# Diagonals spread by GpSimd instead of ScalarE for units 0 to 7 of a recurrent-attention and MLP kernel, with new engine sequences

## The chip, the cores and the metric

One core of a Trainium2 chip runs the whole program. The metric is the device time of one execution in microseconds, and lower is better. The kernel before takes 484.99 us (median of 3 runs, 484.72 to 485.08).

## What is computed

The reference has two parts. The first is a recurrence over 768 tokens for 4 batches and 8 heads of width 48: a state of 48x48 per head is multiplied by a decay `w` and takes in `k v`, and each token reads it with `r`, adding its own `k v` weighted by `u`. The second is an MLP on the 3072 tokens, with an ELU between.

```python
for t in range(S):
    cur = np.einsum('bhd,bhe->bhde', u[None] * kt, vt)
    y[:, :, t] = np.einsum('bhd,bhde->bhe', rt, state + cur)
    state = wt[:, :, :, None] * state + np.einsum('bhd,bhe->bhde', kt, vt)
...
h = x @ w_in                      # 384 -> 2048
g = np.where(h > 0.0, h, np.exp(np.minimum(h, 0.0)) - 1.0)
out = g @ w_out                   # 2048 -> 384
```

Each token's own term is `sum(r u k) v`. In matrix form it is the diagonal of a token by token matrix, and this diagonal is what the change is about.

## The kernel before

The tokens are cut into 24 **units** (unit 0 to 23), four to each of six chunks of 512 token columns. Units 0 to 3 hold 128 tokens of one batch (`whole`), the later ones two halves of 64 tokens. The MLP of a chunk goes over 16 blocks `f` of 128 hidden columns, in 103 steps in all. The first six blocks of chunk 0 are cut in two halves, so that they can begin when units 0 and 1 alone are done.

The names in the sequences are tasks, with the number of the unit, block or step behind the dot. Those that the prediction speaks of:

- `es.i`, `gs.i` (L461, L470, L471): two scans over the decays of unit i on VectorE, with a small reciprocal ahead of the second. `rh.i` (L476) multiplies k and r by them.
- `rkc.i` (L495) then `pd.i` (L500) then `md.i` (L504): for units 0 to 3 the sums r u k as a product on VectorE, a small matmul on TensorE into PSUM, and a copy to the SBUF tile `md` on ScalarE. For the later units `rk.i`, `rku.i`, `md.i` (L483, L486, L490) on VectorE give `md`.
- `sp.i`: the **spread**. It writes the 128 by 8 values of `md` onto diagonals in the tile `ams`, with zeros around them. Units 0 to 7 do it on ScalarE, `spread_act` (L518): eight instructions, each an identity matrix scaled by one column of `md`. Units 8 to 23 do it on GpSimd, `spread` (L529): two affine selects of 64x512 that read `md` broadcast.
- `s.i` (L563, L570): transposes and scores on TensorE. `mk.i` (L599, L601, L605), the **mask**: VectorE copies the scores above the diagonal from PSUM into `ams`. It needs `s.i` and `sp.i`. `v.i` (L550, L640): TensorE multiplies `ams` by the values and makes the state's update. `xf`, `xh`, `xl` copy its result into the MLP's input.
- `a.f`, `cc.f` (L235), `wh.f`, `wl.f` (L731): the weights of block f are unpacked and split into a high and a low part, on ScalarE and VectorE by turns. `wh.0` and `wh.1` are casts on GpSimd (L727). `big.f` (L734) is a check on the weights for which nothing on TensorE waits.
- `g1.n`, `g2.n` (L263, L267; L295, L298): the MLP's matmuls of step n. Between them `r1`, `r2` (ScalarE), `stt` (VectorE, L277, one input from PSUM), `gh` (ScalarE) and `gl` (VectorE, L285).

What sets the order is the table `SEQUENCE` (L80): one list of tasks for each engine and for the DMA queue on SyncE. An engine takes its tasks in the order of its list and waits at each for what it needs. A small planner (`Plan.order`, L170) merges the five lists into program order by the numbers in `COST`, and `hold` says how many buffers a tile has. `FILL` (L44) puts matmuls of ones on TensorE ahead of a task (`warm`, L424), 36 of them in the first 25 us; their result is not used.

```python
def spread_act(u_):
    am = diagonal(u_)
    for q in range(2):
        for p in range(NP):
            act(am[:, q, p], ident if u_["whole"] else ident_h, AF.Copy, scale=u_["md"][:, q, p:p + 1])
```

Of the kernel before, what the change touches and what calls it, by code (L numbers as in the profile page):

```python
# [95 lines left out]
rh.3 stt.3 wl.3 cc.4 es.4 es.5 gl.3 wl.4 cc.5 mk.3 stt.4 wl.5 stt.5 rk.4 gl.4 big.3 cc.6 stt.6 gs.4 gl.5 xl.3 gl.6 xl.2 rku.4 stt.7 md.4 stt.8 cc.7
wl.6 rh.4 stt.9 sc.4 rk.5 gl.9 cc.8 gs.5 rku.5 stt.10 md.5 stt.11 rh.5 wl.7 mk.4 wl.8 gl.11 gl.10 cc.9 sc.5 rk.6 stt.12 stt.13 xl.4 es.6 up.4 rku.6
gl.13 gl.12 cc.10 gs.6 mk.5 stt.14 wl.9 gl.14 rh.6 cc.11 stt.15 md.6 wl.10 rk.7 wl.11 cc.12 gl.15 stt.16 up.5 xl.5 rku.7 es.7 sc.6 cc.13 stt.17 wl.12
gl.16 mk.6 md.7 cc.14 gs.7 gl.17 sc.7 stt.18 rh.7 wl.13 stt.19 up.6 wl.14 es.9 gl.18 xl.6 cc.15 stt.20 es.8 gl.19 wl.15 rk.8 mk.7 sc.8 stt.21 gs.9
gl.20 gl.21 rk.9 rku.8 xl.7 gs.8 rku.9 rh.8 stt.22 md.8 md.9 rh.9 gl.22 up.7 stt.23 tn.9 es.10 rk.10 gl.23 sc.9 stt.24 gs.10 rh.10 gl.24 stt.25 tn.10  # L100
es.11 rk.11 gl.25 rku.11 mk.8 big.10 stt.27 stt.26 md.11 rku.10 md.10 up.8 gs.11 gl.27 gl.26 mk.9 sc.10 rh.11 es.12 stt.28 big.11 rk.12 gl.28 xl.8
stt.29 gs.12 big.2 stt.30 up.9 tn.11 mk.10 gl.29 sc.11 rh.12 stt.31 xl.9 es.13 gl.30 gl.31 wl.1 wl.0 rku.12 gs.13 md.12 es.14 rk.13 stt.32 gl.32
rku.13 up.10 stt.33 gs.14 gl.33 tn.12 stt.34 sc.12 rk.14 rh.13 xl.10 stt.35 mk.11 gl.34 md.13 rku.14 gl.35 es.15 big.9 tn.13 stt.36 mk.12 rh.14 gl.36
# [36 lines left out]
ld_w.0 ld_k.0 ubd ld_w.1 ld_k.1 raw.0 ld_v.0 ld_w.2 ld_k.2 raw.1 ld_v.1 ld_w.3 raw.2 raw.3 ld_k.3 raw.4 ld_v.2 ld_w.4 ld_w.5 raw.5 ld_v.3 raw.6  # L140
# [983 lines left out]
```

## Time and profile before

| | before |
|---|---|
| median of 3 runs | 484.99 us (484.72 to 485.08) |
| the profiled execution | 486.13 us |
| its span, first to last instruction | 484.4 us |
| TensorE busy | 475.7 us (98%) |
| VectorE busy | 359.1 us (74%) |
| ScalarE busy | 260.4 us (54%) |
| GpSimd busy | 40.7 us (8%) |
| granted TensorE clock | 1.000 over the span |

The profiled execution took 1.73 us more than its span, and 1.14 us more than the median of the runs. Busy shares are averages over stages: the first 40 us, in which weights are unpacked and the first units are made, are unlike the rest. A matmul that is in flight counts as busy, so TensorE is read here by its waits and by when a given matmul starts.

### The profile page before, as it was taken

The numbers are of one execution on the slowest core, as the hardware profiler recorded it, in microseconds if no ns is written. First come the engines' busy times: TensorE is split into PE (matmuls) and PEld (weight loads), VectorE is DVE, ScalarE is ACT, GpSimd is POOL, SyncE is SP. The second block draws the span as 40 slices with busy tenths as digits, with TensorE's granted clock in tenths as the row PEclk, the third lists the DMA queues.
The fourth block names the chain that finished last, engine by engine and source line by source line (L and its number), as shares of the span: only waits on it lengthen the run. The fifth ranks groups of instructions, "written<-read, shape, count | busy, mean of one in ns | idle before, by whom it ended". The sixth has DMA issues, their size and how long they took to land.

```text
span 484.4 us, 12143 instructions
## 1 busy us (share of the span) xinstructions
PE 475.7 (98%) x4978; PEld 395.3 (82%) x4978; DVE 359.1 (74%) x545; ACT 260.4 (54%) x535; POOL 40.7 (8%) x56
## 2 busy tenths in 40 slices
PE   9999999999999999999999999999999999999996
PEld 8888888878888787788788878888888888888885
DVE  7999999999899999979997896655426453333332
ACT  4998878856544443635343643536544343644442
POOL 3000000004011302012101101101001000000000
PEclk9999999999999999999999999999999999999999
DMA  8999477417485664855754747332521100100001
GB/s 276 363 319 293 149 250 244 146 41 205 89 260 129 187 141 117 241 146 104 209 156 107 216 101 207 89 87 81 133 59 39 38 2 1 65 2 0 0 2 66
DMA packets 75418, 64.91 MB, mean 134 GB/s; under 512 B 56976, under 2 KB 57360, under 8 KB 75360
## 3 DMA queue, kind: packets, MB, share of 16 engines
q1 hardware_dynamic: 74784, 63.33, 46.3%
q8 instruction: 39, 0.64, 0.6%
q10 hardware_dynamic: 576, 0.79, 0.5%
q14 instruction: 19, 0.16, 0.1%
HBM read 49.67 MB, written 8.13 MB: 119 GB/s over the span
## 4 chain that ended last, share of the span: by engine, by line
PE 75%; DVE 16%; issue 3%; DMA 3%; ACT 2%; DVEq 0%; POOL 0%; POOLq 0%
PE ph L267 32%; PE acc L298 31%; PE py L550 2%; PE px L570 2%; PE acc L426 2%; DVE ams L605 2%; DVE m L277 2%; PE px L550 2%; DVE gl L285 2%; DVE eg L461 2%; DMA w<-in_wkr_dram 1%; DVE k L476 1%; PE px L640 1%; DVE tops L734 1%; DMA k<-in_wkr_dram 1%
## 5 line engine op out<-in xcount | busy, mean ns | idle before, releaser
L271 ACT ACTIVATE m<-ph 128x512 f32<-128x512 f32 (+2 forms) x103 | 58.3, 567 | 102.0 <-PE ph L267 69.8
L267 PE MATMUL ph<-xh,w_l 128*128 128x512 f32 (+1 forms) x294 | 112.0, 381 | 0.0
L298 PE MATMUL acc<-gh,w_l 128*128 128x512 f32 (+1 forms) x292 | 111.2, 381 | 0.0
L277 DVE SCALAR_TENSOR_TENSOR m<-m,ph 128x512 f32<-128x512 f32 (+2 forms) x103 | 66.2, 646 | 57.2 <-ACT m L274 56.6
L281 ACT CAST gh<-m 128x512 fp32r<-128x512 f32 (+1 forms) x98 | 58.9, 602 | 86.6 <-PE acc L298 60.4
L267 PE MATMUL ph<-xh,w_h 128*128 128x512 f32 (+1 forms) x264 | 102.5, 388 | 1.8 <-DVE m L277 1.4
L298 PE MATMUL acc<-gh,w_h 128*128 128x512 f32 (+1 forms) x264 | 102.3, 388 | 0.0
L285 DVE TENSOR_TENSOR gl<-m,gh 128x512 fp32r<-128x512 f32 (+1 forms) x98 | 67.0, 690 | 46.3 <-ACT gh L281 45.1
L298 PE MATMUL acc<-gl,w_h 128*128 128x512 f32 (+1 forms) x264 | 100.4, 380 | 0.3 <-DVE gl L285 0.3
L267 PE MATMUL ph<-xl,w_h 128*128 128x512 f32 (+1 forms) x264 | 100.3, 380 | 0.0
L267 PEld LDWEIGHTS ph<-xh,w_l 128*128 128x128 f32 x294 | 55.3, 188 | 10.8
L298 PEld LDWEIGHTS acc<-gh,w_l 128*128 128x128 f32 x292 | 54.9, 188 | 10.5
L274 ACT ACTIVATE m<-m 128x512 f32<-128x512 f32 (+2 forms) x103 | 61.2, 601 | 1.7
L267 PEld LDWEIGHTS ph<-xh,w_h 128*128 128x128 f32 x264 | 49.6, 188 | 13.8 <-DVE m L277 3.3
L298 PEld LDWEIGHTS acc<-gh,w_h 128*128 128x128 f32 x264 | 49.6, 188 | 10.3
L298 PEld LDWEIGHTS acc<-gl,w_h 128*128 128x128 f32 x264 | 49.6, 188 | 9.7 <-DVE gl L285 0.7
L267 PEld LDWEIGHTS ph<-xl,w_h 128*128 128x128 f32 x264 | 49.7, 188 | 8.9
L529 POOL TENSOR_SCALAR_AFFINE_SELECT ams<-md 64x512 f32<-64x512 f32 x32 | 32.1, 1002 | 242.2 <-PE py L550 164.2
L461 DVE TENSOR_TENSOR_SCAN eg<-w,reset 112x520 f32<-112x520 f32 (+1 forms) x24 | 30.1, 1256 | 2.8 <-DMA w<-in_wkr_dram 2.8
L471 DVE TENSOR_TENSOR_SCAN eg<-w,reset 112x520 f32<-112x520 f32 (+1 forms) x24 | 30.3, 1263 | 0.8
L476 DVE TENSOR_TENSOR k<-k,eg 112x1024 f32<-112x1024 f32 x24 | 29.1, 1214 | 0.1
L605 DVE COPY_PREDICATED ams<-upper_h,px 64x512 f32<-64x512 uint32 x32 | 23.5, 735 | 1.4 <-PE px L570 0.9
(127 smaller groups left out, 501.6 us busy)
## 6 DMA issues: line engine op xcount, KB each, us to landing
wraw<-in_wraw_dram SPq DMA_DIRECT2D x16, 767.8 KB, 6.6
rk<-in_rk_dram SPq DMA_DIRECT2D x20, 384.0 KB, 4.5
k<-in_wkr_dram SPq DMA_DIRECT2D x13, 512.0 KB, 4.3
w<-in_wkr_dram SPq DMA_DIRECT2D x24, 227.9 KB, 4.1
k<-in_wkr_dram SPq DMA_DIRECT2D x11, 448.0 KB, 5.5
wide<-in_vp_dram SPq DMA_DIRECT2D x32, 128.0 KB, 4.0
...
```

Of the source, the lines that this page charges most:

```text
L267: nc.tensor.matmul(ph, w[f][:, 0, k], y[:, k], start=(k == n == 0), stop=(k == NK - 1 and n == 2))
L271: act(s["m"], s["ph"], AF.Relu, scale=-1.0)
L274: act(s["m"], s["m"], AF.Exp, scale=-1.0)
L277: stt_(s["m"], s["m"], -1.0, s["ph"], ALU.add, ALU.max)
L281: nc.scalar.copy(s["gh"], s["m"])
L285: nc.vector.tensor_tensor(s["gl"], s["m"], s["gh"].bitcast(F32), ALU.subtract)
L298: nc.tensor.matmul(a_, w[f][:, 1, m], fold(s, g[:, a:b]), start=(first and n == 0), stop=(final and n == 2))
L461: nc.vector.tensor_tensor_scan(out=eg[:, 0, 0:n][:, ::-1], data0=u_["w"][:, 1:n + 1][:, ::-1], data1=reset[:, 0, 0:n][:, ::-1], initial=0. ...
L471: nc.vector.tensor_tensor_scan(out=u_["eg"][:, 1, 1:n + 1], data0=u_["w"][:, 0:n], data1=reset[:, 1, 0:n], initial=0.0, op0=ALU.mult, op1= ...
L476: tt(t, t, u_["eg"][:, :, 0:u_["n"]].rearrange("d z (s t) -> d z s t", t=u_["L"] + 1)[..., 1:], ALU.mult)
L529: nc.gpsimd.affine_select(out=am[rs, h].rearrange("t q p s -> t (q p) s"), in_=u_["md"][rs].rearrange("t q p -> t (q p)").unsqueeze(2).bro ...
L605: nc.vector.copy_predicated(u_["am"][rs, h], above[L][rs], pa[rs])
```

## The change

The spread of units 0 to 7 moves from ScalarE to GpSimd. `spread_rows` writes units 0 to 3 with one affine select of 128x1024, and units 4 to 7 with two of 64x512. The sums `pd.i` get PSUM columns of their own, 448 to 463 of the bank `py`, two sets by turns, where before they shared columns 0 to 7 with the transposes. The task `s.i` no longer names `sp.i` among the tasks that it comes after; the mask `mk.i` still does. All five lists of `SEQUENCE` are new, and so is `FILL`, now 40 matmuls of ones.

```diff
-FILL = {("pd",0):17,("s",0):5,("pd",1):3,("s",1):2,("v",1):8,("s",2):1,("g2",0):0}
+FILL = {("pd",0):19,("s",0):3,("pd",1):2,("v",0):3,("v",1):10,("g1",1):3,("g2",0):0}
...
-SPREAD = ["ACT"] * 8 + ["POOL"] * 16
+SPREAD = ['ROWS'] * 8 + ['POOL'] * 16
...
     def diag_pe(u_):
-        u_["pd"] = pd = single()[:, 0:NS].rearrange("t (p z) -> t p z", p=NP)
+        lo = NP * R2 + NS * (u_["i"] % 2)
+        u_["pd"] = pd = single()[:, lo:lo + NS].rearrange("t (z p) -> t z p", p=NP)
         for p in range(NP):
-            nc.tensor.matmul(pd[:, p], u_["rkc"][:, p, :], ubd[:, p, :], start=True, stop=True)
+            nc.tensor.matmul(pd[:, :, p], u_["rkc"][:, p, :], ubd[:, p, :], start=True, stop=True)
...
-    def spread_act(u_):
-        am = diagonal(u_)
-        for q in range(2):
-            for p in range(NP):
-                act(am[:, q, p], ident if u_["whole"] else ident_h, AF.Copy, scale=u_["md"][:, q, p:p + 1])
...
+    def spread_rows(u_):
+        am, n = diagonal(u_).rearrange("t q p s -> t (q p) s"), u_["L"]
+        for lo in range(0, C, n):
+            rs = slice(lo, lo + n)
+            nc.gpsimd.affine_select(out=am[rs], in_=u_["md"][rs].rearrange("t q p -> t (q p)").unsqueeze(2).broadcast_to([n, NS, n]),
+                                    pattern=[[0, NS], [1, n]], compare_op=ALU.is_equal, fill=0.0, base=0, channel_multiplier=-1)
...
-                [("rh", i), ("const",)] + [("sp", i)] * (i > 1) + before * (not new))
+                [("rh", i), ("const",)] + before * (not new))
...
-            hold("pb", ("pd", i), [("md", i)], fifo=False)
+            hold("pd", ("pd", i), [("md", i)])
```

Three places show how the lists moved. The first is VectorE from `rh.3` to `mk.3`, the mask of unit 3, before:

```order
L476 TENSOR_TENSOR k_295<-k_295,eg_372 112x1024
L277 SCALAR_TENSOR_TENSOR m_463<-m_463,ph_441 128x256
L731 TENSOR_TENSOR w_l_103<-wg_435,w_h_102 128x768
L235 SCALAR_TENSOR_TENSOR wg_510<-wraw_299,top_117 128x768
L461 SCALAR_TENSOR_TENSOR eg_525<-w_325,reset_104 112x520
L461 SCALAR_TENSOR_TENSOR eg_545<-w_395,reset_104 112x520
L285 TENSOR_TENSOR gl_550<-m_463,gh_530 128x256
L731 TENSOR_TENSOR w_l_103<-wg_510,w_h_102 128x768
L235 SCALAR_TENSOR_TENSOR wg_568<-wraw_411,top_117 128x768
L599 COPY_PREDICATED ams_114<-upper_108,px_115 128x512 x2
```

and the same stretch now:

```order
L477 TENSOR_TENSOR k_282<-k_282,eg_345 112x1024
L278 SCALAR_TENSOR_TENSOR m_420<-m_420,ph_404 128x256
L278 SCALAR_TENSOR_TENSOR m_445<-m_445,ph_425 128x256
L730 TENSOR_TENSOR w_l_103<-wg_413,w_h_102 128x768
L236 SCALAR_TENSOR_TENSOR wg_487<-wraw_289,top_117 128x768
L462 SCALAR_TENSOR_TENSOR eg_504<-w_384,reset_104 112x520
L730 TENSOR_TENSOR w_l_103<-wg_487,w_h_102 128x768
L236 SCALAR_TENSOR_TENSOR wg_525<-wraw_387,top_117 128x768
L286 TENSOR_TENSOR gl_539<-m_445,gh_485 128x256
L598 COPY_PREDICATED ams_114<-upper_108,px_115 128x512 x2
```

One of the two scans (`es.4`) has gone behind the mask; `stt.2` has moved here from just ahead of `mk.2`. From the first scan to `mk.3` everything else is the same set of tasks.

The second place is VectorE's first unit, now (L462 and L472 are scans, L496 is `rkc`, L477 is `rh`):

```order
L462 SCALAR_TENSOR_TENSOR eg<-w,reset 112x516 x2
L471 RECIPROCAL reset<-eg 112x4
L472 SCALAR_TENSOR_TENSOR eg<-w,reset 112x516
L496 TENSOR_TENSOR rkc<-k 112x512
L477 TENSOR_TENSOR k<-k,eg 112x1024
L471 RECIPROCAL reset<-eg 112x4
L472 SCALAR_TENSOR_TENSOR eg<-w,reset 112x516
L496 TENSOR_TENSOR rkc<-k 112x512
L598 COPY_PREDICATED ams<-upper,px 128x512 x2
```

The first row's second instruction, `es.1`, now stands ahead of `gs.0` and `rkc.0`; before it stood behind both.

The third place is GpSimd's list behind its constants, now:

```order
L409 MEMSET st 112x1280
L521 AFFINE_SELECT ams<-md 128x1024 x2
L388 MEMSET reset 112x1040
L389 MEMSET reset 112x8
L521 AFFINE_SELECT ams<-md 128x1024 x2
L534 MEMSET wide 32x512
L521 AFFINE_SELECT ams<-md 64x512 x8
L534 MEMSET wide 32x512 x2
L528 AFFINE_SELECT ams<-md 64x512 x2
L726 CAST w_g<-wt 128x768
L528 AFFINE_SELECT ams<-md 64x512 x4
L726 CAST w_g<-wt 128x768
```

The rows at L521 are new there, and the two casts `wh.1` and `wh.0`, which stood one behind the other, now have two units' spreads between them.

## Rows read from the trace of the kernel before

**Rows 1.** Busy time by stretch: us, then each engine's busy us (x instructions), clock, DMA share, GB/s.

```profile
5.00:10.00 5.00, 5.00 (x39) 4.86 (x38) 4.90 (x8) 1.48 (x7) 0.00 (x0) 1.00 1.04 357
...
35.00:40.00 5.00, 4.01 (x66) 3.39 (x66) 5.00 (x10) 4.01 (x9) 0.00 (x0) 1.00 1.02 392
```

**Rows 2.** All of VectorE's waits in the first 100 us: total us, times, longest.

```profile
DVE eg L461 <- DMA w<-in_wkr_dram: 1.4, 1, 1.4
DVE reset L387 <- PEq L1111: 1.1, 1, 1.1
DVE ams L601 <- PE px L550: 0.6, 1, 0.6
```

**Rows 3.** All of TensorE's waits from 40 us on, same columns.

```profile
PE ph L267 <- DVE m L277: 1.4, 2, 1.0
PE px L550 <- issue: 1.0, 1, 1.0
PE ph L267 <- DVE reset L470: 0.2, 1, 0.2
```

**Rows 4.** Instructions at L518, the spread on ScalarE: duration min/median/max, and who waited.

```profile
L518 ACT ACTIVATE ams<-ident,md x32: 384/388/404, 8.8 to 32.4; 128x128 f32<-128x128 f32 x32
...
  ACT m L271: 0.4, 1
```

**Rows 5.** VectorE in order of time: start us, us, instruction.

```profile
6.50 0.67 DVE L495 TENSOR_TENSOR rkc<-k 112x512 f32<-112x512 f32 x1
...
9.55 1.23 DVE L471 TENSOR_TENSOR_SCAN eg<-w,reset 112x516 f32<-112x516 f32 x1
10.70 0.67 DVE L495 TENSOR_TENSOR rkc<-k 112x512 f32<-112x512 f32 x1
11.50 1.35 DVE L599 COPY_PREDICATED ams<-upper,px 128x512 f32<-128x512 uint32 x2
...
32.79 2.37 DVE L461 TENSOR_TENSOR_SCAN eg<-w,reset 112x520 f32<-112x520 f32 x2
35.07 0.40 DVE L285 TENSOR_TENSOR gl<-m,gh 128x256 fp32r<-128x256 f32 x1
...
37.13 1.35 DVE L599 COPY_PREDICATED ams<-upper,px 128x512 f32<-128x512 uint32 x2
```

**Rows 6.** TensorE and ScalarE in order of time: unit 0, and the values of unit 3.

```profile
7.53 0.95 PE L500 MATMUL py<-ubd,rkc 112*128 112x2 f32 x8
...
8.52 0.17 ACT L504 COPY md<-py 128x8 f32<-128x8 f32 x1 [6.41 <-PE py L500]
...
38.54 0.73 PE L550 MATMUL px<-ams,wide 128*32 128x128 f32 x17 [0.72 <-DVE ams L599]
```

**Rows 7.** Instructions at L529, the spread on GpSimd: duration min/median/max, first and last.

```profile
L529 POOL TENSOR_SCALAR_AFFINE_SELECT ams<-md x32: 651/657/2092, 111.7 to 367.1; 64x512 f32<-64x512 f32 x32
```

**Rows 8.** Groups of GpSimd's instructions: count, busy us, mean ns of one, idle before.

```profile
masks.py:199 POOL TENSOR_SCALAR_AFFINE_SELECT ident<-ident 128x128 f32<-128x128 f32 x1 | 0.3, 293 | 0.1
```

**Rows 9.** One spread and VectorE beside it, in order of time.

```profile
224.86 3.40 POOL L529 TENSOR_SCALAR_AFFINE_SELECT ams<-md 64x512 f32<-64x512 f32 x2 [16.41 <-PE py L550]
...
225.06 0.55 DVE L486 TENSOR_TENSOR rk<-rk,ub 128x384 f32<-128x384 f32 x1
225.53 0.68 DVE L285 TENSOR_TENSOR gl<-m,gh 128x512 fp32r<-128x512 f32 x1
226.13 1.68 DVE L461 TENSOR_TENSOR_SCAN eg<-w,reset 112x520 f32<-112x520 f32 x1
```

**Rows 10.** The two casts of GpSimd, VectorE beside them, and TensorE behind, in order of time.

```profile
162.66 2.06 POOL L727 CAST w_g<-wt 128x768 fp32r<-128x768 f32 x2
...
162.70 1.33 DVE L285 TENSOR_TENSOR gl<-m,gh 128x512 fp32r<-128x512 f32 x1 [0.74 <-ACT gh L281]
163.95 1.18 DVE L486 TENSOR_TENSOR rk<-rk,ub 128x384 f32<-128x384 f32 x1
...
166.25 0.50 PE L267 MATMUL ph<-xh,w_h 128*128 128x512 f32 x1 [0.98 <-DVE m L277]
```

More of the change, by code (lines that the diff above doesn't have):

```diff
@@ L96 @@
[L96 to L103, printed above, removed]
@@ L112 @@
-mk.22 gl.76 xl.21 stt.77 stt.78 up.21 gl.77 sc.23 gl.78 stt.79 least gl.79 stt.80 stt.81 gl.80 gl.81 mk.23 verdict stt.82 gl.82 xl.22 stt.84 stt.83
-gl.84 gl.83 stt.85 xl.23 stt.86 gl.85 gl.86 stt.87 gl.87 stt.88 gl.88 stt.89 gl.89 stt.90 gl.90 stt.91 stt.92 gl.91 gl.92 stt.93 gl.93 stt.94 stt.95
-gl.94 gl.95 stt.96 gl.96 stt.97 stt.98 gl.97 gl.98 stt.99 gl.99 stt.100 gl.100 stt.101 stt.102 gl.101 gl.102 end.1 end.2 end.3
+es.0 es.1 gs.0 rkc.0 rh.0 gs.1 rkc.1 mk.0 rh.1 es.2 cc.0 gs.2 rkc.2 mk.1 rh.2 stt.0 es.3 cc.1 gs.3 cc.2 xl.1 xl.0 stt.1 wl.2 cc.3 rkc.3 mk.2 rh.3
@@ new lines @@
+rh.8 gl.21 xl.7 rku.8 sc.8 rk.9 stt.22 up.7 md.8 es.10 gl.22 gs.9 rku.9 stt.23 rh.9 gs.10 stt.24 gl.23 tn.9 wl.1 gl.24 md.9 rh.10 sc.9 stt.25 mk.8
+gl.25 stt.26 es.11 tn.10 gs.11 rk.10 es.12 rk.11 stt.27 gl.26 rku.10 up.8 gs.12 mk.9 gl.27 stt.28 md.10 rh.11 stt.29 gl.28 xl.8 big.15 wl.0 rku.11
+es.13 tn.11 mk.10 stt.30 sc.10 md.11 gl.29 rh.12 gs.13 gl.30 stt.31 up.9 rk.12 stt.32 tn.12 rh.13 gl.31 rku.12 sc.11 es.14 big.11 xl.9 stt.33 gs.14
+gl.32 big.10 md.12 stt.34 gl.33 rk.13 mk.11 stt.35 rku.13 up.10 big.14 gl.34 tn.13 rh.14 stt.36 xl.10 es.15 gl.35 md.13 sc.12 rk.14 xl.11 up.11 gl.36
@@ L115 @@
+mk.22 stt.75 sc.23 gl.75 stt.76 gl.76 stt.77 gl.77 mk.23 stt.78 gl.78 stt.79 xl.22 stt.80 gl.79 stt.81 gl.80 stt.82 gl.81 gl.82 stt.83 least gl.83
+stt.84 gl.84 xl.23 stt.85 gl.85 stt.86 gl.86 stt.87 stt.88 gl.87 gl.88 stt.89 stt.90 gl.89 stt.91 gl.90 verdict stt.92 gl.91 gl.92 stt.93 gl.93 stt.94
+gl.94 stt.95 gl.95 stt.96 gl.96 stt.97 gl.97 stt.98 stt.99 gl.98 gl.99 stt.100 gl.100 stt.101 stt.102 gl.101 gl.102 end.1 end.2 end.3
 """,
     ACT="""
-md.0 pc.1 sp.0 pc.0 kt.0 a.0 md.1 sp.1 xf.0 up.0 kt.1 xh.0 r1.0 a.1 md.2 sp.2 r2.0 xf.1 a.2 r1.1 up.1 xh.1 r2.1 wh.2 a.3 pc.3 kt.2 r1.2 r2.2 pc.2 wh.3
@@ L135 @@
+r2.85 gh.84 r1.86 gh.85 r2.86 gh.86 r1.87 r2.87 gh.87 r1.88 r2.88 out.4.0 out.4.1 r1.89 gh.88 out.4.2 r2.89 r1.90 r2.90 gh.89 r1.91 r2.91 gh.90 gh.91
+r1.92 r2.92 r1.93 r2.93 gh.92 r1.94 gh.93 r2.94 r1.95 gh.94 r2.95 gh.95 r1.96 r1.97 r2.96 gh.96 r2.97 gh.97 r1.98 r2.98 r1.99 r2.99 gh.98 r1.100 gh.99
+r2.100 r1.101 gh.100 r2.101 r1.102 r2.102 gh.101 gh.102 part end.0
 """,
     POOL="""
-const reset.4 clear.0 clear.1 clear.2 sp.9 sp.8 sp.10 sp.11 sp.12 wh.1 wh.0 sp.13 sp.14 sp.15 sp.16 sp.17 sp.18 sp.19 sp.20 sp.21 sp.22 sp.23
+const sp.0 sp.1 reset.4 sp.2 sp.3 clear.0 sp.4 sp.5 sp.6 sp.7 clear.1 clear.2 sp.8 wh.1 sp.9 sp.10 wh.0 sp.11 sp.12 sp.13 sp.14 sp.15 sp.16 sp.17
@@ L138 @@
+sp.18 sp.19 sp.20 sp.21 sp.22 sp.23
 """,
     SP="""
[L140 to L142 removed]
@@ L150 @@
+ld_wx.2 store.3.1 ld_wx.4 ld_wx.6 store.4.1 store.4.2 guard store.4.0
 """,
```

121 lines of the change are left out of this document (58 added, 63 removed).

## The prediction

> **What bounds the kernel now.** I read the busy time by stretch first, then the waits of VectorE and of TensorE, and then the first 40 us in order of time. In the stretches [rows 1] look at the third busy number, VectorE: 4.90 of 5.00 us at 5 to 10 us, and all of 35 to 40 us. Its waits over the first 100 us [rows 2] are 3.1 us in all, and 2.5 of them come before it has a decay to scan. So from its first scan on VectorE has work at nearly every moment, and whatever the first units need from it comes when its list has got there. TensorE's busy number means less early, since it also runs matmuls of ones; what shows its state is the matmul of `v.3` at 38.54 us [rows 6], which waited for VectorE's mask `ams`, and the 35 to 40 us stretch [rows 1], where TensorE has 4.01 of 5.00 us. Behind it TensorE is full: all its waits from 40 us on are 2.6 us [rows 3]. Its work behind `v.3` is the same before and after the change.
>
> So the time is the moment of `v.3`, plus a fixed amount of TensorE work, plus its few waits. ScalarE, which the change relieves, sets none of these: of the 64 instructions of the spread there (32 of them 388 ns each), only 0.4 us of waiting hangs on them, and that is another ScalarE task [rows 4]. Eight make a unit, at most 8 x 0.388 = 3.1 us of ScalarE for each of the first four, and I give that relief **nothing**: the masks that need a spread come out of VectorE's list later than the spread is ready. The cover is VectorE's own backlog; were it gone, ScalarE's relief could be worth some tenths. That `s.i` no longer comes behind `sp.i` is worth nothing for the same reason, as are the PSUM columns of `pd.i`: both let TensorE be early for a mask that is late.
>
> **The change part by part.** I follow VectorE from its first scan to `mk.3`.
>
> *The moved scan.* `es.4` goes behind `mk.3`. Two scans started at 32.79 us and the next instruction at 35.07 us [rows 5], so one is 2.28 / 2 = 1.14 us. It has to be done before `gs.4`, well behind `v.3`, where TensorE has steps of its own to run: **-1.14 us**.
>
> *Unit 0.* `es.1` now stands ahead of `rkc.0`, so `rkc.0`, which ended at 6.50 + 0.67 = 7.17 us [rows 5], ends about 1.0 us later (a scan, less a pause that it fills), at 8.2 us. Its sums left TensorE at 7.53 + 0.95 = 8.48 us [rows 6], 1.3 us behind it, and the copy to `md` ended at 8.52 + 0.17 = 8.69 us [rows 6]; now that is 9.7 us, and the spread can ask at 9.8 us. I need the length of a 128x1024 select, which the trace doesn't show. A 128x128 one took 0.293 us [rows 8] and a 64x512 one at least 0.651 us [rows 7]; (0.651 - 0.293) / 384 columns is 0.93 ns each, so 1024 columns are 0.651 + 512 x 0.93 ns = **1.13 us** undisturbed, an estimate from these two rows.
>
> But it won't be undisturbed. The spreads' durations run from 0.651 to 2.092 us with the same shape [rows 7]. In [rows 9] a select that comes at 224.86 us, two in a row lasting 3.40 us, stands through a product of two SBUF tiles (225.06) and another (225.53); then the scan at 226.13 takes 1.68 us instead of the 1.23 us of [rows 5], 0.45 us more. The casts say it again [rows 10]: beside them `gl` takes 1.33 us, where the same kind at 225.53 took 0.68 us, and `rku` 1.18 us where it took 0.55 us at 225.06 [rows 9], so 0.65 and 0.63 us more, and TensorE then waits 0.98 us at 166.25 us. GpSimd reading SBUF and VectorE reading two SBUF tiles shut each other out, one instruction at a time. A mask or `stt` reads PSUM and one SBUF tile, and I take it as open to GpSimd.
>
> The spread of unit 0 comes at 9.8 us in the middle of `gs.1`, which runs from 9.55 us to 10.7 us, with `rkc.1` behind it [rows 5]. If it goes in between, it ends at 11.85 us, `rkc.1` at 12.3, and the mask starts at 12.35 us; if `rkc.1` passes it, it runs from 11.3 to 12.45 us and the mask starts at 12.5 us. Before, it started at 11.50 us [rows 5]. The Trainium skill (SBUF — State Buffer, Who interferes with whom) says that the two engines share a port pair as an exclusive lock, and that whichever issues first has it. The trace agrees on the lock; on the order [rows 9] differ, as a waiting select was passed by two products. By the page the term is +0.85, by the row +1.0, and the sum would differ by 0.15 us. I take **+0.9**. The lowest is +0.4 (in between, and `rkc.1` not held up), the highest +1.0.
>
> *Units 1 to 3.* A select that goes in between two port users costs VectorE its length less what an instruction start hides: 0.45 us of 0.65 us above, so about 0.2 us hidden, and 0.93 us here. For unit 1 there is hardly a way round: from `mk.0` to `mk.1` the list is `rh.1`, `es.2`, `cc.0`, `gs.2`, `rkc.2`, all port users: +0.9. Unit 2 can go in beside `stt.1` or where VectorE waits for ScalarE: +0.6. Unit 3 can hide under `mk.2` or under `stt.2`, `stt.3`, which now stand together: +0.3. Together **+1.8**; nothing at best, since half the selects so far were not stretched (the median of [rows 7] is 0.657 us), and 3 x 0.93 = 2.8 us at worst.
>
> `v.3` then comes 0.9 + 1.8 - 1.14 = 1.6 us later, at about 40.1 us.
>
> *Units 4 to 7.* Eight selects of 64x512, two per unit. Behind each `md` VectorE's next is an `stt`, under which the first can hide; the second meets port users and costs 0 to 0.45 us. At 0.2 us each that is 0.8 us of VectorE, and I pass half on to TensorE, which has some work ahead there: **+0.4**, between 0 and 4 x 0.45 = 1.8 us.
>
> *TensorE's waits behind 40 us.* The two casts are taken apart, so their 1.3 us no longer fall on one spot. Of the 1.4 us that TensorE waited for `stt` [rows 3], I give back **-0.6**. The 1.0 us put down to issue has no cause that I can see, and I leave it. The lists are new throughout, with the DMA queue's order: I can't follow 390 us of them, and bound this by all 2.6 us of [rows 3] gone, less 0.2, or by one more wait like that at 166.25 us: -2.4 to +1.2. The 4 more matmuls of ones, and the ten ahead of `v.1`, stand where TensorE waits for a mask.
>
> The sum is -1.14 + 0.9 + 1.8 + 0.4 - 0.6 = **+1.36 us**. Against the profiled execution (486.13 us, a span of 484.4 and 1.73 around it) that would be 487.5 us; the median of the runs lies 1.14 us under that execution, so I predict 484.99 + 1.36, **486.3 us**.
>
> **The rivals.** *VectorE is not held up (faster).* The selects find the masks, the `stt` and the small pauses, and GpSimd is the one that waits. For it: half of the 32 spreads were not stretched at all [rows 7]. Against it: those ran where VectorE also had masks, `stt` and reductions; the first 40 us are scans, products and unpacking. Then the front is -1.14 + 0.4 = -0.7, the waits behind it -0.6 to -2.4: about 483.1 us. It decides at the point where the delay of VectorE before `mk.3`, unit 0 included, is under 1.14 us.
>
> *A draw.* The delay just eats the moved scan, ScalarE's relief is worth nothing, TensorE was full behind 40 us and stays so: 485.0 us. For it: [rows 3]. A kernel whose TensorE waits so little can't gain much.
>
> *GpSimd is starved (slower still).* If it is passed again and again, as in [rows 9], each mask of units 1 to 3 stands and waits the whole 1.13 us, and those of units 4 to 7 0.65 us: -1.14 + 1.0 + 3.4 + half of 2.6 = +4.6, less the 0.6: 489.0 us. Against it: no select waited more than 1.5 us so far.
>
> *The change doesn't do what it says*, since ScalarE was no bound: that is the draw.
>
> **How the numbers follow.** About 0.2% (1 us) is what a measurement of this kernel can tell from no change. Chances: VectorE held up, as forecast, 0.36; starved 0.08; a draw 0.22; not held up 0.34. The forecast's own range, with the bounds of unit 0 and of the first three selects, is 485.2 to 488.2 us. For 8 in 10 I take in the faster case down to 482.8 us (front -0.7, waits -1.5) and go up to 488.5 us. Slower by over 0.2% has 0.44, within 0.2% 0.22, faster 0.34.
>
> **What would show it.** In the changed kernel's trace: a 128x1024 select of 1.13 us where nothing stands beside it, longer elsewhere; scans and products of VectorE in the first 40 us stretched from 1.23 or 0.67 us to about 2.0 or 1.5 us, three or four of them; `mk.0` at 12.3 to 12.5 us; `v.3` near 40.1 us against 38.54 us; the two casts apart with no wait of 1 us behind them; VectorE still without waits. If `v.3` comes before 38.5 us with no VectorE instruction stretched, the port term is wrong. If it comes at 40 us and the kernel is still no slower, the end is not set by `v.3`, and the new lists won it back later: then TensorE's waits behind 40 us are under 1 us.

## The result and the profile after

The changed kernel takes 490.18 us (median of 4 runs, 488.90 to 491.03), the kernel before 485.03 us in the same series (484.72 to 485.10). The ratio is 1.0106 (95% interval 1.0087 to 1.0125): slower by 5.15 us, where +1.36 us was forecast, and outside the range of 482.8 to 488.5 us. The profiled execution of the changed kernel took 488.90 us with a span of 486.8 us.

The busy time by stretch, in the columns of [rows 1]:

```profile
5.00:10.00 5.00, 4.11 (x36) 3.92 (x35) 4.74 (x8) 0.46 (x3) 0.30 (x1) 1.00 0.99 283
35.00:40.00 5.00, 4.70 (x43) 4.04 (x43) 5.00 (x7) 4.15 (x8) 1.28 (x1) 1.00 1.04 293
```

ScalarE at 5 to 10 us went from 1.48 to 0.46 us and GpSimd has work, so the change does what it says. VectorE still fills 35 to 40 us, but with 7 instructions where it had 10. GpSimd's select and VectorE beside it show why:

```profile
9.70 1.09 POOL L521 TENSOR_SCALAR_AFFINE_SELECT ams<-md 128x1024 f32<-128x1024 f32 x1 [4.86 <-ACT md L515]
14.27 1.50 POOL L521 TENSOR_SCALAR_AFFINE_SELECT ams<-md 128x1024 f32<-128x1024 f32 x1 [3.48 <-ACT md L515]
...
26.69 1.60 POOL L521 TENSOR_SCALAR_AFFINE_SELECT ams<-md 128x1024 f32<-128x1024 f32 x1
34.47 1.81 POOL L521 TENSOR_SCALAR_AFFINE_SELECT ams<-md 128x1024 f32<-128x1024 f32 x1 [6.18 <-ACT md L515]
```

```profile
9.71 2.17 DVE L472 TENSOR_TENSOR_SCAN eg<-w,reset 112x516 f32<-112x516 f32 x1
11.80 0.66 DVE L496 TENSOR_TENSOR rkc<-k 112x512 f32<-112x512 f32 x1
12.38 1.33 DVE L598 COPY_PREDICATED ams<-upper,px 128x512 f32<-128x512 uint32 x2
...
14.74 2.11 DVE L462 TENSOR_TENSOR_SCAN eg<-w,reset 112x516 f32<-112x516 f32 x1
...
27.45 1.65 DVE L730 TENSOR_TENSOR w_l<-wg,w_h 128x768 fp32r<-128x768 f32 x1
...
35.26 2.12 DVE L462 TENSOR_TENSOR_SCAN eg<-w,reset 112x520 f32<-112x520 f32 x1
...
39.35 1.35 DVE L598 COPY_PREDICATED ams<-upper,px 128x512 f32<-128x512 uint32 x2
```

VectorE's waits in the first 100 us are much as in [rows 2], but for new ones, of which these are the two longest; both come behind 40 us:

```profile
DVE m L278 <- ACT m L275: 1.0, 2, 0.6
DVE ams L600 <- POOL ams L521: 0.6, 1, 0.6
```

Each of the four selects stretches one VectorE instruction with two SBUF inputs: three scans (1.23 us undisturbed, [rows 5]) by 0.94, 0.88 and 0.89 us, and one split of weights (0.95 us undisturbed) by 0.70 us, 3.41 us in all. Less the 1.14 us of the moved scan that is 2.27 us. `v.3` starts at 40.81 us against 38.54 us [rows 6], 2.27 us later as well:

```profile
40.81 0.96 PE L549 MATMUL px<-ams,wide 128*32 128x128 f32 x26
```

All of TensorE's waits from 40 us on, in the columns of [rows 3], and the place of the first in order of time:

```profile
PE px L549 <- issue: 1.9, 1, 1.9
PE acc L299 <- DVE gl L286: 0.7, 1, 0.7
```

```profile
59.04 0.33 PE L549 MATMUL px<-k,st 48*32 48x64 f32 x8
61.30 0.42 PE L549 MATMUL px<-k,st 48*32 48x64 f32 x22 [1.93 <-issue]
```

The sum, 2.6 us, is that of before, but one wait of 1.9 us now stands inside `v.4`, in the midst of 30 like matmuls, and no engine ends it. A profiled execution is one of several: the four runs have mean granted clocks of 0.999, 1.000, 0.997 and 0.996 and take 488.90, 489.36, 491.00 and 491.03 us. The two with the lower clock are 2 us longer. The profiled one is of the first sort; and the profiled one of before lay 1.14 us above its median. So the pair of profiles shows 486.8 - 484.4 = 2.4 us of the 5.15.

### The profile page after: what moved, and what is told of

It is laid out like the page before. It is cut to its first block, busy times and chain, and to the rows that moved or that the text cites. A ratio compares the mean times of both kernels' runs of the same rounds, so it can differ in the third digit from the quotient of the medians.

```text
span 486.8 us, 12114 instructions
## 1 busy us (share of the span) xinstructions
PE 476.8 (98%) x4986; PEld 396.0 (81%) x4986; DVE 362.5 (74%) x545; ACT 242.7 (50%) x471; POOL 57.8 (12%) x68
## 4 chain that ended last, share of the span: by engine, by line
PE 85%; DVE 8%; DMA 3%; issue 2%; SPq 1%; ACT 0%; DVEq 0%
PE acc L299 38%; PE ph L268 37%; PE py L549 3%; PE px L569 2%; PE px L549 2%; PE px L639 1%; DMA k<-in_wkr_dram 1%; DVE k L477 1%; DVE eg L462 1%; DVE eg L472 1%; DVE m L278 1%; DMA rows<-turn 1%; DMA w<-in_wkr_dram 1%; DVE wg L236 1%; DVE w_l L730 1%
## 5 line engine op out<-in xcount | busy, mean ns | idle before, releaser
L286 DVE TENSOR_TENSOR gl<-m,gh 128x512 fp32r<-128x512 f32 (+1 forms) x98 | 65.5, 669 | 58.3 <-ACT gh L282 58.0
L528 POOL TENSOR_SCALAR_AFFINE_SELECT ams<-md 64x512 f32<-64x512 f32 x32 | 33.4, 1042 | 201.9 <-PE py L549 87.6
L462 DVE TENSOR_TENSOR_SCAN eg<-w,reset 112x520 f32<-112x520 f32 (+1 forms) x24 | 32.6, 1360 | 1.6 <-DMA w<-in_wkr_dram 1.6
L472 DVE TENSOR_TENSOR_SCAN eg<-w,reset 112x520 f32<-112x520 f32 (+1 forms) x24 | 31.7, 1321 | 0.8
L477 DVE TENSOR_TENSOR k<-k,eg 112x1024 f32<-112x1024 f32 x24 | 30.2, 1257 | 0.3 <-DMA k<-in_wkr_dram 0.3
```

The source lines that it names most:

```text
L286: nc.vector.tensor_tensor(s["gl"], s["m"], s["gh"].bitcast(F32), ALU.subtract)
L462: nc.vector.tensor_tensor_scan(out=eg[:, 0, 0:n][:, ::-1], data0=u_["w"][:, 1:n + 1][:, ::-1], data1=reset[:, 0, 0:n][:, ::-1], initial=0. ...
L472: nc.vector.tensor_tensor_scan(out=u_["eg"][:, 1, 1:n + 1], data0=u_["w"][:, 0:n], data1=reset[:, 1, 0:n], initial=0.0, op0=ALU.mult, op1= ...
L477: tt(t, t, u_["eg"][:, :, 0:u_["n"]].rearrange("d z (s t) -> d z s t", t=u_["L"] + 1)[..., 1:], ALU.mult)
L528: nc.gpsimd.affine_select(out=am[rs, h].rearrange("t q p s -> t (q p) s"), in_=u_["md"][rs].rearrange("t q p -> t (q p)").unsqueeze(2).bro ...
```

## The experiments

Two causes were to be told apart. **P**: GpSimd reading SBUF shuts VectorE out. **C**: TensorE waits in `v.4` for its own instructions, and then runs for a while at a lower clock. Against both stood **S**: the new sequences are worse in themselves. The texts on record say what each theory forecasts. All times, with ratios to the kernel before in the same series; its own median went from 484.96 to 485.72 us between the series, so kernels of different series are compared by their ratios. In the kernel before `v.3` starts at 38.54 us.

| kernel | median us (range, runs) | ratio to before (95%) | `v.3` starts, us |
|---|---|---|---|
| changed kernel | 490.18 (488.90 to 491.03, 4) | 1.0106 (1.0087 to 1.0125) | 40.81 |
| act_first_four | 490.82 (488.99 to 493.37, 6) | 1.0113 (1.0086 to 1.0140) | 41.32 |
| rows_in_old_lists | 490.08 (488.12 to 491.90, 6) | 1.0098 (1.0072 to 1.0124) | 40.69 |
| write_only_select | 487.51 (486.24 to 488.75, 12) | 1.0039 (1.0026 to 1.0052) | 37.80 |
| fewer_ones | 489.64 (488.12 to 490.74, 6) | 1.0080 (1.0057 to 1.0102) | 40.59 |
| v4_later | 488.53 (487.64 to 489.12, 6) | 1.0066 (1.0049 to 1.0083) | 40.54 |
| write_only_v4_later | 485.26 (484.62 to 488.56, 12) | 1.0006 (0.9991 to 1.0021) | 38.10 |
| select_twice | 492.87 (491.92 to 494.73, 5) | 1.0158 (1.0134 to 1.0182) | 43.75 |
| scan_behind_mask | 484.92 (484.81 to 486.61, 12) | 0.9996 (0.9984 to 1.0007) | 37.65 |
| scan_and_check_later | 485.46 (484.82 to 487.75, 12) | 1.0002 (0.9989 to 1.0014) | 37.68 |
| and_casts_apart | 485.51 (484.16 to 485.95, 11) | 1.0000 (0.9991 to 1.0010) | 37.79 |
| four_to_seven_in_old_lists | 486.88 (485.81 to 489.65, 12) | 1.0029 (1.0012 to 1.0046) | 38.70 |
| both_scans_behind_gl6 | 486.91 (485.59 to 488.43, 12) | 1.0032 (1.0018 to 1.0046) | 37.75 |

### Units 0 to 3 back on ScalarE

```diff
-SPREAD = ['ROWS'] * 8 + ['POOL'] * 16
+SPREAD = ['ACT'] * 4 + ['ROWS'] * 4 + ['POOL'] * 16
```

with `sp.0` to `sp.3` behind `md.0` to `md.3` in the changed kernel's ScalarE list.

> The changed kernel with the spreads of units 0 to 3 back on ScalarE, each right behind its md; units 4 to 7 stay on GpSimd, all lists otherwise those of the change. Theory P (port): the selects of units 0 to 3 shut VectorE's two-input instructions out for about 0.9 to 1.0 us each, which made v.3 2.3 us later than before. Then no VectorE instruction of the first 40 us is stretched, v.3 starts at 37.5 to 38.5 us instead of 40.81, and the time falls by 2 to 3 us, to about 487.5. Theory S (the new lists are worse in themselves): v.3 stays at 40 us or later and the time within 1 us of 490. Theory C (TensorE waits for its code inside v.4): it says nothing of v.3; the wait of about 2 us inside v.4 stays or moves, as the count of TensorE's instructions ahead of it is unchanged I expect it to stay.

No better: 490.82 us, and `v.3` at 41.32 us. That is what theory S forecast, and P's forecast of `v.3` at 37.5 to 38.5 us failed; the wait in `v.4` stayed, as C expected, with 2.7 us. No VectorE instruction of the first 40 us is stretched any more, but its waits in the first 100 us have new heads:

```profile
DVE w_l L736 <- ACT w_h L724: 3.3, 2, 2.0
DVE m L278 <- ACT m L275: 1.7, 2, 1.3
```

The new ScalarE list has no room for the spread there, and VectorE waits for ScalarE's weights instead. So this run doesn't undo one part alone, and it can't tell P from S; the next one does. It suggests that the new sequences have used up ScalarE's relief.

### The selects in the old sequences

```diff
-SPREAD = ["ACT"] * 8 + ["POOL"] * 16
+SPREAD = ["ROWS"] * 8 + ["POOL"] * 16
```

in the kernel before, with `sp.0` to `sp.7` taken from ScalarE's list to GpSimd's and no other move.

> The kernel before with its own lists, and only the spreads of units 0 to 7 taken from ScalarE's list and put on GpSimd's, with the change's affine selects. Theory P: the selects stretch VectorE as in the changed kernel, v.3 starts 2.5 to 3.5 us later than 38.54 us (no scan is moved away here), and the time rises by 2.5 to 4.5 us, to 487.5 to 489.5. Theory S: the time stays within 1 us of before. Theory C: TensorE has the same instructions in the same order as before, so its waits for code stay those of before; no part of a rise comes from them.

A loss of the same size came in the old lists, 490.08 us (ratio 1.0098), so S fails as its cause. `v.3` starts at 40.69 us, and scans are stretched again:

```profile
9.76 1.91 DVE L472 TENSOR_TENSOR_SCAN eg<-w,reset 112x516 f32<-112x516 f32 x1
...
15.39 2.11 DVE L462 TENSOR_TENSOR_SCAN eg<-w,reset 112x516 f32<-112x516 f32 x1
```

Unit 2's select stretched nothing, since it ran beside a mask:

```profile
19.58 1.09 POOL L530 TENSOR_SCALAR_AFFINE_SELECT ams<-md 128x1024 f32<-128x1024 f32 x1 [3.16 <-ACT md L505]
```

```profile
19.36 1.32 DVE L607 COPY_PREDICATED ams<-upper,acc 128x512 f32<-128x512 uint32 x2
```

The other three cost two scans and a split 0.68, 0.88 and 0.58 us, 2.14 in all, and `v.3` is 2.15 us later than in the kernel before. P had forecast 2.5 to 3.5 us there, too much. By 60 us TensorE's work stands 3.0 us later, and its wait for instructions in `v.7`, 1.0 us before [rows 3], is 1.4 us here, where C had said that it would stay the same. (Of the 2.2 us put down to issue in this line of the trace, 0.75 stand at `v.3` itself, where the mask had just ended.) So the sum is near that of the changed kernel, but not its terms: here there is no wait in `v.4`, and units 4 to 7 cost more, as shown further down.

### A spread that writes and doesn't read

```diff
     def spread_rows(u_):
         am, n = diagonal(u_).rearrange("t q p s -> t (q p) s"), u_["L"]
+        if u_["whole"]:
+            nc.gpsimd.memset(am, 0.0)
+            return
```

> The changed kernel with the select of units 0 to 3 replaced by a memset of the same 128x1024 tile, so GpSimd writes as much but reads nothing of SBUF; the diagonals of these four units are left out of the result. Theory P, if only reading SBUF shuts VectorE out: no stretched scans in the first 40 us, v.3 at 37.5 to 38.5 us, time 2 to 3 us less than the changed kernel. If GpSimd's writes shut VectorE out too, or if the delay comes from the masks waiting for the spread: v.3 stays near 40.8 us and the time near 490. Theory S: no difference to the changed kernel.

The fills don't read `md`, so they also run earlier than the selects, two of them at 25 us. GpSimd, and VectorE beside these two:

```profile
25.02 1.84 POOL L520 MEMSET ams<- 128x1024 f32 x2
```

```profile
24.67 1.02 DVE L692 TENSOR_TENSOR xl<-wide,xh 128x384 fp32r<-128x384 f32 x2
25.61 0.28 DVE L278 SCALAR_TENSOR_TENSOR m<-m,ph 128x128 f32<-128x128 f32 x1
25.81 0.95 DVE L733 TENSOR_TENSOR w_l<-wg,w_h 128x768 fp32r<-128x768 f32 x1
```

The split `w_l`, with two SBUF inputs, lies inside the fills and takes 0.95 us; beside a select it took 1.65 us. The other two ran at 4.77 us beside the scans of `es.0` and `es.1`, which took 2.36 us for the two, as in the changed kernel where nothing stands beside them. It is the reading that shuts VectorE out. The Trainium skill (SBUF — State Buffer, Who interferes with whom) says just that: a VectorE instruction with two SBUF inputs contends with a GpSimd instruction that reads SBUF, not with one that only writes it. These rows agree. `v.3` starts at 37.80 us, 3.0 us earlier than in the changed kernel, and the ratio falls from 1.0106 to 1.0039, some 3.2 us. The rest is still there, and this trace shows two parts of it, the wait and the clock. The granted clock (behind the busy time of TensorE) in three stretches:

```profile
40.00:59.60 19.60, 17.76 (x297) 1.00 0.62 211
59.60:63.00 3.40, 3.40 (x16) 0.50 0.74 226
63.00:70.00 7.00, 7.00 (x41) 1.00 0.78 240
```

TensorE stood from 56.36 to 58.20 us in `v.4`, as in the changed kernel, then worked, and from 59.60 us ran at 1.2 of its 2.4 GHz for 3.4 us: half of that, 1.7 us, is lost. Of the 12 runs the four at 0.999 or 1.000 take 486.24 to 486.87 us, and of the eight at 0.996 or less all but one take 487.50 to 488.75 us. By these times the six at 0.996 are 0.9 us longer on average than the four, which is less than the 1.7 us.

### Fewer matmuls of ones

```diff
-FILL = {("pd",0):19,("s",0):3,("pd",1):2,("v",0):3,("v",1):10,("g1",1):3,("g2",0):0}
+FILL = {("pd",0):19,("s",0):3,("pd",1):2,("v",0):0,("v",1):4,("g1",1):0,("g2",0):0}
```

> The changed kernel with 12 of its 40 matmuls of ones left out (none ahead of v.0 and g1.1, four ahead of v.1), that is 48 instructions fewer on TensorE ahead of v.4, whose result nothing used. TensorE waits for a mask at these places anyway. Theory C: its code comes in pieces of 16 KB, a piece began to load 0.4 us ahead of the wait of 1.93 us inside v.4, and 48 instructions fewer put the end of the piece elsewhere: the wait inside v.4 goes or falls by over 1 us, and the time falls by 1 to 2 us or more, with runs that agree better. It may come up in another unit's values. Theories P and S: no change in v.3 (40.8 us, 0.3 us either way) nor in the time (within 0.7 us).

```profile
58.82 0.54 PE L549 MATMUL px<-k,st 48*32 48x64 f32 x30
59.29 0.38 PE L268 MATMUL ph<-xh,w_h 128*128 128x256 f32 x1
61.75 0.28 PE L268 MATMUL ph<-xl,w_h 128*128 128x256 f32 x1 [2.07 <-issue]
```

`v.4` now runs through, and the wait stands between two matmuls of the next step that read tiles long ready. It kept its place in TensorE's count of instructions, not in the work. The fall of the wait by over 1 us, which C had forecast as well, did not come, `v.3` stayed as P and S had it, and the time, 1.3 us less than the changed kernel's by the ratios, tells nothing, since the two intervals overlap. Beside it lies a transfer of the trace's instruction queue, the second row here of the page's queues of the changed kernel:

```profile
q1 hardware_dynamic: 74784, 63.33, 47.3%
q8 instruction: 39, 0.64, 0.6%
```

39 pieces of 16 KB. Where such a piece begins to load, when TensorE reaches the instruction at which it waits (matmuls and weight loads counted from the start), and when it goes on:

| kernel | load begins, us | instruction | reached, us | goes on, us |
|---|---|---|---|---|
| before | 102.88 | 2983 | 104.3 | 105.52 |
| rows_in_old_lists | 106.71 | 2983 | 107.4 | 109.08 |
| four_to_seven_in_old_lists | 104.75 | 2983 | 105.5 | 107.12 |
| scan_and_check_later | 102.81 | 2983 | 104.2 | 105.19 |
| and_casts_apart | 102.92 | 2983 | 104.4 | 105.29 |
| scan_behind_mask (no wait) | 101.86 | 2983 | 104.3 | 104.3 |
| both_scans_behind_gl6 (no wait) | 103.16 | 2983 | 105.5 | 105.5 |
| changed kernel | 58.74 | 1453 | 59.2 | 61.30 |
| act_first_four | 60.17 | 1451 | 59.7 | 62.53 |
| write_only_select | 55.53 | 1453 | 56.1 | 58.20 |
| fewer_ones | 59.30 | 1451 | 59.4 | 61.75 |
| select_twice | 62.54 | 1453 | 62.1 | 65.08 |
| v4_later (no wait) | 59.50 | 1451 | 62.3 | 62.3 |

In the ten traces with a wait TensorE goes on 2.4 to 2.7 us after the load's beginning, whatever the matmul is. In the changed kernel the last 254 instructions before the wait, from the end of `s.4`'s burst over two steps into `v.4`'s, went by from 55.34 to 59.14 us, in 3.8 us; in the kernel before the same count there took 5.7 us, without a wait. So short matmuls close together can outrun the load. They don't do it every time: at 2983 the last 254 took 3.8 to 3.9 us in all seven kernels with TensorE's old order, and two of them had no wait, since there the load began at the 2753rd instruction, in the five others at the 2760th to 2872nd. What sets that moment, the runs don't show. The 1.0 us of issue in [rows 3] is one of these waits, and from there to the end the trace of scan_behind_mask is 1.2 us ahead of that of before. The Trainium skill (Runtime: NRT & Kernel Launch, Instruction fetch mechanics) calls the cost at the edge of such a block of 256 instructions mostly hidden. Here it was 0.7 to 2.8 us where it was not hidden.

### The two bursts further apart

```diff
-g2.8 s.4 g1.11 g2.9 v.4 g1.12 g2.10 g1.13
+g2.8 s.4 g1.11 g2.9 g1.12 g2.10 v.4 g1.13
```

> The changed kernel with one task moved: v.4 goes behind g2.10 on TensorE (before it stood ahead of g1.12), so that the two bursts of small products s.4 and v.4 lie two big steps further apart; xh.4 goes behind r2.12 on ScalarE. Nothing is left out. Theory P+C (VectorE shut out by GpSimd's reads, +2.3 us; and a wait of 1.9 to 2.1 us of TensorE for its instructions in v.4, with a lower granted clock behind it in some executions, some 2 us more): the wait behind v.4's first products is gone or under 0.5 us, the granted clock stays at 1.0, v.3 still starts 2.0 to 2.4 us later than in the kernel before, and the time is 486.5 to 488.5 us. Rival P alone (the wait in v.4 would be made up later, the rest of the loss lies elsewhere): 489.5 to 491 us with the wait gone. Rival D (the wait is for v.4's data): the wait goes with v.4 and stands at its new place.

All of TensorE's waits from 40 us on:

```profile
PE acc L299 <- DVE gl L286: 1.3, 2, 0.9
```

The wait is gone, not moved, and the time is 488.53 us, at the upper end of what P and C together forecast; by the ratios it is 1.9 us less than the changed kernel's. Five of the six runs have a clock of 0.999 or 1.000, against two of four. A third of the wait came back, as 0.6 us more of waiting for `gl`.

### Both removed

This is the write-only spread with the move of `v.4`.

> The last kernel and the write-only spread together: the selects of units 0 to 3 become fills of the same tile with zeros, so the diagonals of these four units are left out of the output. Theory P+C: both losses are gone, v.3 starts 0.5 to 1 us earlier than in the kernel before, no wait over 1 us is left behind it, and the time is 483.5 to 485.5 us, at or under the kernel before. Rival L (the new sequences behind 40 us are themselves worse): 486.5 to 488 us.

485.26 us, no different from before (0.9991 to 1.0021). By differences of the ratios, the reads are worth 1.0106 - 1.0039 = 0.0067, or 3.2 us, with the wait in place and 1.0066 - 1.0006 = 0.0060, or 2.9 us, without it; the wait, with the clock behind it, 1.0106 - 1.0066 = 0.0040, or 1.9 us, with the reads and 1.0039 - 1.0006 = 0.0033, or 1.6 us, without. By the intervals each is good to about 1 us. Both together are 0.0100, or 4.85 of the 5.15 us. What is left on, the new sequences with units 4 to 7 on GpSimd, comes out even with the kernel before.

### The select twice

```diff
-        for lo in range(0, C, n):
+        for lo in [0, 0] if u_["whole"] else range(0, C, n):
```

> The changed kernel with each select of units 0 to 3 issued twice; the second writes the same values again. Theory P: each further select shuts VectorE out for 0.7 to 0.95 us wherever one of its scans or splits of two SBUF inputs stands, so VectorE's stretched instructions add 2.5 to 3.8 us more, v.3 starts 4.5 to 6 us later than in the kernel before, and the time is 492.5 to 494.5 us. Rival Q (only the first collision of a unit is on the path, since VectorE has slack between its tasks): v.3 under 1 us later than in the changed kernel and 490 to 491.2 us.

```profile
9.35 2.17 DVE L472 TENSOR_TENSOR_SCAN eg<-w,reset 112x516 f32<-112x516 f32 x1
11.44 1.50 DVE L496 TENSOR_TENSOR rkc<-k 112x512 f32<-112x512 f32 x1
12.87 1.33 DVE L598 COPY_PREDICATED ams<-upper,px 128x512 f32<-128x512 uint32 x2
```

The second select hits the next product: `rkc.1` takes 1.50 us for 0.67 us. The second selects of the other three units hit one instruction each as well, for 0.68, 0.89 and 0.89 us. `v.3` starts 2.9 us later than in the changed kernel, and the time is 2.5 us more by the ratios, as P forecast. VectorE has no slack to take a second collision either.

### The moved scan, the later units and the casts by themselves

`scan_behind_mask` is the kernel before with `es.4` behind `mk.3`:

```diff
-cc.4 es.4 es.5 gl.3 wl.4 cc.5 mk.3 stt.4 wl.5 stt.5 rk.4
+cc.4 es.5 gl.3 wl.4 cc.5 mk.3 stt.4 wl.5 stt.5 es.4 rk.4
```

> The kernel before with one task moved: es.4 goes behind mk.3 and the two instructions after it on VectorE. This is the term of -1.14 us of the prediction by itself. By that term mk.3 and v.3 start 1.0 to 1.2 us earlier than in the kernel before, and the time is 483.6 to 484.4 us. Rival R (what mk.3 waits for, the scores or the spread, comes last, or the scan is only late later, before rh.4): v.3 moves by under 0.5 us, or the gain is given back by v.4, and the time is 484.6 to 485.6 us.

TensorE in order of time:

```profile
37.65 1.08 PE L550 MATMUL px<-ams,wide 128*32 128x128 f32 x32 [0.38 <-DVE ams L599]
...
43.15 0.70 PE L263 MATMUL ph<-wide,w_f 128*128 128x256 f32 x2 [0.28 <-DVE m L277]
```

`v.3` starts 0.89 us earlier, and by 51 us nothing of it is left: `stt.6`, `gl.5` and `gl.6` stand behind the scan as they did before, so they come no earlier, and TensorE waits for them. The rival held. Two further kernels tried to keep the gain. The first puts `es.4` behind `gl.5`, `gs.4` behind `xl.3`, and `big.3` far back:

```diff
-mk.3 stt.4 wl.5 stt.5 rk.4 gl.4 big.3 cc.6 stt.6 gs.4 gl.5 xl.3 gl.6
+mk.3 stt.4 wl.5 stt.5 rk.4 gl.4 cc.6 stt.6 gl.5 es.4 xl.3 gs.4 gl.6
```

> The kernel before with three tasks of VectorE moved: es.4 goes behind gl.5 and gs.4 behind xl.3, so that mk.3 no longer waits for a scan of 1.1 us, and big.3 (0.9 us, for which nothing on TensorE waits) goes from behind gl.4 to behind stt.33; pc.4 goes behind r2.7 on ScalarE. In the last run the scan alone behind the mask made v.3 0.9 us earlier, and the products at 43 and 47 us, which wait for VectorE, gave it back. If VectorE's total of work ahead of these products is what took it back, v.3 starts 0.8 to 1.0 us earlier than in the kernel before, 0.6 to 1.0 of it is still there at 55 us, and the time is 483.9 to 484.4 us. Rival (TensorE's later waits are set by something else than VectorE's start): the gain is gone by 60 us again and the time is 484.7 to 485.3 us.

The gain lasted to 45 us; then ScalarE waited for `gl.6`, which stood behind both scans:

```profile
45.59 0.38 ACT L271 ACTIVATE m<-ph 128x256 f32<-128x256 f32 x1 [1.42 <-DVE gl L285]
```

`and_casts_apart` is that kernel with the casts taken apart in GpSimd's list (and `wl.1` earlier on VectorE):

```diff
-sp.9 sp.8 sp.10 sp.11 sp.12 wh.1 wh.0 sp.13
+sp.9 sp.8 sp.10 sp.11 wh.1 sp.12 wh.0 sp.13
```

> The last kernel, and the two casts of GpSimd apart as in the changed kernel: wh.1 goes ahead of sp.12, and wl.1, which it needs, behind stt.29 on VectorE. This is the term of -0.6 us of the prediction by itself. By that term the wait of 1.0 us near 166 us is under 0.5 us and the time is 0.4 to 0.8 us under the last kernel's. Rival: the wait moves to another product near 158 to 170 us and nothing is gained.

485.51 against 485.46 us: no gain. The wait for `stt` went from 1.3 to 0.4 us in the profiles, that for `gl` from 0.2 to 0.8. The rival held.

`four_to_seven_in_old_lists` is the kernel before with only `sp.4` to `sp.7` on GpSimd:

> The kernel before with the spread of units 4 to 7 alone moved to GpSimd (two selects of 64x512 each), units 0 to 3 left on ScalarE; the lists are otherwise those of before. This is the term of +0.4 us of the prediction by itself: 485.2 to 485.6 us, with three to six VectorE instructions stretched by 0.3 to 0.9 us each but TensorE waiting for at most one of them. Rival (VectorE's delay comes through whole): 486 to 487 us. Rival (ScalarE's relief of 8.5 us in a stretch where its tasks lie between TensorE's steps is worth something): 484 to 484.7 us.

486.88 us, 1.0029 (1.0012 to 1.0046), some 1.4 us. The two selects of unit 4, and what VectorE has beside them:

```profile
47.39 1.98 POOL L530 TENSOR_SCALAR_AFFINE_SELECT ams<-md 64x512 f32<-64x512 f32 x2 [0.73 <-DVE md L491]
```

```profile
47.57 1.27 DVE L236 SCALAR_TENSOR_TENSOR wg<-wraw,top 128x768 uint32<-128x768 uint32 x1
48.77 1.40 DVE L739 TENSOR_TENSOR w_l<-wg,w_h 128x768 fp32r<-128x768 f32 x1
```

0.96 and 0.95 us before, so 0.76 us more at unit 4, and a product at 56.66 us, beside unit 5's, was stretched by 0.33 us. At 60 us TensorE's work stands 1.05 us later than in the kernel before, 0.9 of it since `v.3`: these two units came through nearly whole. Units 6 and 7 stretched VectorE by another 1.48 us, four instructions from 77.63 us on, but at 104 us TensorE is only 1.17 us late. The other 0.4 us is TensorE's wait for instructions in `v.7`, 1.4 us for the 1.0 of [rows 3].

So in the old lists the four units stretch VectorE by 2.57 us. In the changed kernel it is 0.17, 0.45 and 0.14 us, 0.76 in all (undisturbed: 1.23 us for the scans, 1.22 for the product):

```profile
54.60 1.40 DVE L472 TENSOR_TENSOR_SCAN eg<-w,reset 112x520 f32<-112x520 f32 x1
...
77.63 1.67 DVE L477 TENSOR_TENSOR k<-k,eg 112x1024 f32<-112x1024 f32 x1
...
83.09 1.37 DVE L462 TENSOR_TENSOR_SCAN eg<-w,reset 112x520 f32<-112x520 f32 x1
```

Here the new sequences are the better ones.

`both_scans_behind_gl6` is the second trial to keep the scan's gain, made from `and_casts_apart`:

```diff
-cc.6 stt.6 gl.5 es.4 xl.3 gs.4 gl.6 xl.2 rku.4 stt.7
+cc.6 stt.6 gl.5 gl.6 es.4 xl.3 gs.4 xl.2 rku.4 stt.7
```

> The last but one kernel (es.4 and big.3 later, casts apart) with one more step: es.4 and gs.4 go behind gl.6 on VectorE, since there ScalarE waited 1.4 us for gl.6, which stood behind these two scans, and this took back v.3's gain of 0.85 us by 51 us. If that queue was the whole loss, 0.6 to 0.9 us are still there at 60 us, and the time is 0.6 to 0.9 us under that kernel's 485.5, or 0.3 to 1.2 us under the kernel before. Rival (the scores of unit 4, for which both scans are needed, come next): gone again by 54 us, and the time is that of the kernel before within 0.3 us.

Slower, 1.0032, which neither theory had. `stt.7` now stands behind both scans, and TensorE waits for it. (The trace is of one of the four fastest executions, 485.77 us, and has no wait in `v.7`; the eight others took 486.60 to 488.43 us.)

```profile
48.25 0.36 PE L267 MATMUL ph<-xh,w_h 128*128 128x256 f32 x1 [1.84 <-DVE m L277]
```

## Why the prediction was right or wrong

**Where the miss lies.** Of 5.15 us, 1.36 were forecast; 3.8 are missing. The reads of units 0 to 3 had +0.9 and +1.8, 2.7 us, and cost 2.9 to 3.2. The wait in `v.4`, with the clock behind it, had nothing and cost 1.6 to 1.9. The rest (the moved scan, units 4 to 7, the casts) had -1.14 + 0.4 - 0.6 = -1.34, and the kernel with both causes removed is 0.3 us slower than the one before. So the forecast failed by a wait that it left out and by two gains that did not come.

**The direction and the path up to `v.3` were right.** VectorE's list sets `v.3`, a select that reads SBUF stretches the two-input instruction beside it, and a delay of `v.3` comes through to the end (2.9 us more there, 2.5 us more in the time, with the select twice). The undisturbed select is 1.09 us, 1.13 were estimated. Unit 1 cost 0.88 us, 0.9 forecast. Three or four stretched instructions were forecast and four came. `mk.0` at 12.38 us, inside 12.3 to 12.5, is in part luck: both orders that were weighed had the select come into `gs.1`, which holds up `rkc.1` or is passed by it; it came 0.01 us ahead of `gs.1` and held up that scan.

**Units 2 and 3 were sized too small.** The step "unit 2 can go in beside `stt.1` (+0.6); unit 3 can hide under `mk.2` or under `stt.2`, `stt.3` (+0.3)" failed: they cost 0.70 and 0.89 us. Unit 3's select came at 34.47 us, when these were done, with `cc.4` and the scan `es.5` next on VectorE. So `v.3` was 2.27 us late instead of 1.6. That a select can hide under a mask is right: unit 2's did in the old lists. On the order, the Trainium skill's rule that whoever issues first has the ports (the section cited) fits unit 0, where the select began 0.01 us ahead of the scan. It doesn't fit unit 1 in the old lists: the select stood from 13.69 us, took 2.73 us and was passed by a product that began at 14.52 us.

**The moved scan was worth nothing at the end.** The step "it has to be done before `gs.4`, well behind `v.3`, where TensorE has steps of its own to run: -1.14 us" failed. In the old lists it holds up to `v.3` (0.89 us), but `stt` and `gl` of the next steps still queue behind the scan, and TensorE waits for them within 13 us. Had `v.3` been the only landmark, this would not have been seen.

**Units 4 to 7** were put at 0.8 us of VectorE, and "I pass half on to TensorE" made it +0.4. In the changed kernel VectorE is stretched by 0.76 us; how much of it reaches TensorE there was not measured. In the old lists it is 2.57 us, and about 1 us reaches TensorE.

**The casts gave nothing.** They were apart, at 126.15 and 149.40 us, with no wait of 1 us behind them, as stated; but the -0.6 us went to other waits when it was tried by itself.

**TensorE's waits behind 40 us hold the largest miss.** The step was "the 1.0 us put down to issue has no cause that I can see, and I leave it". All that the runs show points to one cause, the load of TensorE's own instructions, and with the new lists, where two bursts of short matmuls come closer together, it is 1.9 us, in the trace of the changed kernel. The clock behind it was in no term. With the clock it costs 1.6 to 1.9 us. That the clock's share is caused by the wait was not shown: the low clock stands 1.4 and 0.7 us behind it in two traces and such runs are rarer without the wait, but the second of these traces (the select twice) has it from 14.6 and from 35.1 us too, ahead of the wait.

**ScalarE's relief was worth nothing in the old lists**, as forecast: `v.3` is late there by just what VectorE was stretched, 2.15 and 2.14 us. In the new lists ScalarE could no longer take the spread back (the first experiment).

**Of the rivals**, the starved GpSimd (489.0 us) came nearest in size, but for another reason: no mask of units 1 to 3 waited for a select, and of the later ones two did, 0.6 and 1.27 us, with no wait of TensorE behind them.

**The range** of 485.2 to 488.2 us doesn't follow from the bounds that it names: 0.4 to 1.0 us for unit 0 and 0 to 2.8 for the next three give 484.05 to 487.45 us.

Left open: what sets the moment at which a piece of instructions begins to load, and why the clock falls in some of the runs behind the same wait and not in others. No version beat the kernel before.
